# Second and fourth attention pair in buffers borrowed from the gelu products

## The chip, the cores and the metric

One Trainium2 chip (trn2), one of its cores. The metric is the device time of one execution in microseconds (us), median of the runs; every run quoted was of the fast state or, being on one core, judged against the fastest of its kernel. A ratio is the mean time of one kernel's fast runs over the mean of the other's fast runs of the same rounds, so it is not quite the ratio of the medians quoted beside it. All profile figures are from one profiled execution of each kernel, whose span is some 2 us shorter than the run's time.

## The reference, cut to what matters

```python
# q, k, v: (8 batches, 8 heads, 576, 64) float32
scores = scale * np.matmul(q, k.transpose(0, 1, 3, 2))
thresh = np.max(scores, axis=-1, keepdims=True) - tau
scores = np.where(scores >= thresh, scores, -1e9)
attn   = softmax(scores)                       # exp, sum, divide
x      = (attn @ v), heads side by side        # (4608, 512)
h      = x @ w_in                              # w_in (512, 2048), float64 in memory
g      = h / (1 + np.exp(-1.702 * h))
out    = g @ w_out                             # w_out (2048, 512), float64 in memory
```

## The kernel before

Two heads make a pair, so there are 32 pairs; four pairs are one batch. The feed-forward part runs in nine blocks of 512 rows. The kernel is written as a list of tasks, each with an engine, an estimated cost, a rank, the tasks it comes after and the buffers it takes and gives back. A small simulation at build time starts, on each engine, the ready task of lowest rank whose buffers are free, and the instructions are issued in the order that results. On the chip each engine then keeps that order, so costs and buffer counts change nothing but order and space.

```python
limits = {"psA": 3, "psM": 2, "s_m": 7, "s_t": 2, "io": 3, "xT": 3, "mb": 1,
          "raw0": 1, "raw1": 1, "qkT0": 1, "qkT1": 1, "v_m": 2, "w64": 3, "cv": 2}
...
gT = [const.tile([P, BLK], FP32, name=f"gT{j}") for j in range(NFC)]   # 16 gelu products
kd = [const.tile([P, P], FP32, name=f"kd{i}") for i in range(2)]        # by n % 2
...
# 64 weight pieces, float64 to float32, rank 3.2 to 4.2
a = task("SP", 1.1, rank, load_w, i, take=("w64",), lag=3.5)
a = task("DVE", 0.6, rank, cv_open, i, after=[a], take=("cv",))
m = task("ACT", 0.42, rank, cv_mant, i, after=[a])
e = task("POOL", 0.82, rank, cv_exp, i, after=[a])
a = task("DVE", 0.42, rank, cv_sign, i, after=[e], give=("w64",))
ready_w.append(task("POOL", 0.75, rank, cv_end, i, after=[a, m], give=("cv",)))
...
# pair n, rank n (cut): transposes, scores in 4 tiles and a tail, row maxima,
# subtract (DVE), mask and exponential (ACT), sums and values (PE), place (DVE)
pq = task("DVE", 0.78, r, prep, n, 0, after=[lq], take=("qkT0",), give=("raw0",))
a  = task("PE", ..., scores, n, t, after=[pq, pk] + ..., take=("psA", "psA", "s_m"),
          give=("qkT0", "qkT1") if tail else ())
```

In the traces, `ps` are scores, `s_m` score tiles, `part` the row maxima of a tile, `mb` the spread maxima, `den` and `pv` sums and values, `hps` and `ops` the two feed-forward products. "DVE" is VectorE, "ACT" ScalarE, "POOL" GpSimd, "PE" TensorE.

Of the kernel before, what the change touches and what calls it, by code (L numbers as in the profile page):

```python
# [10 lines left out]
FP32 = mybir.dt.float32  # L11
# [3 lines left out]
ALU = mybir.AluOpType  # L15
# [3 lines left out]
P = 128  # L19
# [10 lines left out]
def kernel(  # L30
# [29 lines left out]
    nc = tc.nc  # L60
    B, H, S, D = q.shape
    d_model, d_ff = moe_w_in.shape
    NPAIR = H // 2
    NKT = 4
# [3 lines left out]
    QB = S // 32  # L68
    BLK = 512
    NBLK = B * S // BLK  # L70
    NDC = d_model // P
    NFC = d_ff // P
# [5 lines left out]
    const = ctx.enter_context(tc.tile_pool(name="const", bufs=1))  # L78
    work = ctx.enter_context(tc.tile_pool(name="work", bufs=2))
# [2 lines left out]

    w_in = const.tile([P, NDC, d_ff], FP32, name="w_in")
    w_out = const.tile([P, NFC, d_model], FP32, name="w_out")
    gT = [const.tile([P, BLK], FP32, name=f"gT{j}") for j in range(NFC)]
    kd = [const.tile([P, P], FP32, name=f"kd{i}") for i in range(2)]
    v_t = [const.tile([P, 2, D], FP32, name=f"v_t{i}") for i in range(2)]
    ones = const.tile([P, D], FP32, name="ones")
# [12 lines left out]
    tasks = []  # L101
    limits = {"psA": 3, "psM": 2, "s_m": 7, "s_t": 2, "io": 3, "xT": 3, "mb": 1,
              "raw0": 1, "raw1": 1, "qkT0": 1, "qkT1": 1, "v_m": 2, "w64": 3, "cv": 2}

    def task(engine, cost, rank, f, *a, after=(), take=(), give=(), lag=0.06):
        tasks.append((engine, cost, rank, f, a, [x for x in after if x is not None],
                      take, give, lag))
        return len(tasks) - 1
# [47 lines left out]
        assert started == len(tasks), (started, len(tasks))  # L156


    raws, vs = {}, {}

    def load_qk(n, which, queue):
        b, hp = divmod(n, NPAIR)
        name, src = (("q", q), ("k", k))[which]
        t = work.tile([P, QB, 32], FP32, name=f"{name}_raw", tag=f"{name}_raw", bufs=1)
        for h in range(2):
            for j in range(2):
                queue.dma_start(
                    out=t[ds(64 * h + 32 * j, 32), :, :],
                    in_=src[b, 2 * hp + h, :, ts(j, 32)].rearrange("(c p) d -> p c d", p=32),
                )  # L170
        raws[n, which] = t
# [18 lines left out]
    cv = {}  # L190
# [63 lines left out]
    mats, sT, stats, mbs, pss = {}, {}, {}, {}, {}  # L254

    def prep(n, which):

        dst = work.tile([P, S], FP32, name="qkT", tag=f"qkT{which}", bufs=1)
        nc.vector.transpose(out=dst, in_=raws.pop((n, which)).rearrange("p c d -> p (c d)"))  # L259
        mats[n, which] = dst  # L260

    def prep_kd(n):
# [29 lines left out]
    def keep(n, t, h):  # L292
        ps = pss[n, t][h]
        if t == NKT:
            st = work.tile([P, S], FP32, name="s_t", tag="s_t", bufs=2)
            o = st
        else:
            if h == 0:
                st = work.tile([P, 2, S], FP32, name="s_m", tag="s_m", bufs=7)
            else:  # L300
                st = sT[n, t]
            o = st[:, h, :]
        sT[n, t] = st
        nc.scalar.copy(out=halves(o), in_=ps[:, :, 0:SH])  # L304
# [43 lines left out]
        stats[n, ALU.max] = f  # L348

    def spread_max(n):  # L350
        mb = work.tile([P, 2, S], FP32, name="mb", tag="mb", bufs=1)
        nc.vector.transpose(  # L352
            out=mb.rearrange("p h s -> p (h s)"),
            in_=stats[n, ALU.max].unsqueeze(2).to_broadcast([P, 2 * QB, 32]),
        )
        mbs[n] = mb

    def sub(n, t):
        mb, s = mbs[n], sT[n, t]
# [173 lines left out]
    ready_w = []  # L533
    for i in range(len(pieces)):
        rank = NPAIR - 0.8 + i / len(pieces)
        if not wide:
            ready_w.append(task("SP", 0.6, rank, load_w, i, lag=2.5))
            continue
        a = task("SP", 1.1, rank, load_w, i, take=("w64",), lag=3.5)
        a = task("DVE", 0.6, rank, cv_open, i, after=[a], take=("cv",))  # L540
        m = task("ACT", 0.42, rank, cv_mant, i, after=[a])
        e = task("POOL", 0.82, rank, cv_exp, i, after=[a])
        a = task("DVE", 0.42, rank, cv_sign, i, after=[e], give=("w64",))
        ready_w.append(task("POOL", 0.75, rank, cv_end, i, after=[a, m], give=("cv",)))

    tau_done = task("DVE", 1.0, -2.0, tau_terms)

# [41 lines left out]
    for n in range(NP):  # L589
        gate = per_pair * (n - LEAD)  # L590
        after = ffn[gate : gate + 1] if gate >= 0 else []
        r = float(n)
        q0, q1 = (nc.sync, nc.scalar) if n == 0 else (nc.sync, nc.sync)
        lq = task("SP", 2.0, r - 2.0, load_qk, n, 0, q0, take=("raw0",), lag=2.0)
        lk = task("SP", 2.0 if n else 0.1, r - 2.0, load_qk, n, 1, q1, take=("raw1",), lag=2.0)
        lv = task("SP", 2.1, r - 1.2, load_v, n, take=("v_m",), lag=2.0)
        pq = task("DVE", 0.78, r, prep, n, 0, after=[lq], take=("qkT0",), give=("raw0",))
        pk = task("DVE", 0.78, r, prep, n, 1, after=[lk], take=("qkT1",), give=("raw1",))
        pd = task("ACT", 0.5, r, prep_kd, n, after=[pk])
        mx = []  # L600
        for t in range(NKT + 1):
            tail = t == NKT
            a = task(
                "PE", 1.1 if tail else 1.2, r, scores, n, t,
                after=[pq, pk] + ([pd] if tail else []) + after,
                take=("psA", "s_t") if tail else ("psA", "psA", "s_m"),
                give=("qkT0", "qkT1") if tail else (),
            )
            after = [a]
            c = [  # L610
                task("ACT", 0.64, r, keep, n, t, h, after=[a], give=("psA",))
                for h in range(1 if tail else 2)
            ]
            mx.append(task("DVE", 0.78 if tail else 1.37, r, in_groups, n, t, ALU.max, after=c))
        a = task("DVE", 0.75, r, over_tiles, n, ALU.max, after=mx)
        a = task("DVE", 0.75, r, over_groups, n, ALU.max, after=[a])
        a = task("DVE", 0.6, r, lower, n, after=[a, tau_done])
        m = task("DVE", 1.38, r, spread_max, n, after=[a], take=("mb",))
        ws, subs = [], [m]
        for t in range(NKT + 1):  # L620
            tail = t == NKT
            a = task(
                "DVE", 1.5 if tail else 1.37, r, sub, n, t, after=subs[-1:],
                give=("mb",) if tail else (),
            )
            subs.append(a)
            a = task("ACT", 0.7 if tail else 1.17, r, mask, n, t, after=[a])
            ws.append(task("ACT", 0.88 if tail else 1.36, r, exps, n, t, after=[a]))
        back = ("s_m",) * NKT + ("s_t",)
        every = range(NKT + 1)  # L630
        if n < NPAIR:

            pv = den = None
            for t in every:
                first = t == 0
                den = task(
                    "PE", 1.1, r, sums_by_pe, n, [t], True, after=[ws[t], den],
                    take=("psM", "psM") if first else (),
                )
                pv = task(  # L640
                    "PE", 1.1, r, values, n, [t], after=[ws[t], den, pv, lv],
                    take=("psA",) if first else (), give=(back[t],) if t < NKT else ("s_t", "v_m"),
                )
            a = task("DVE", 1.2, r, one_row, n, after=[den], give=("psM", "psM"))
        else:
            pv = task("PE", 5.0, r, values, n, every, after=ws + [lv], take=("psA",), give=("v_m",))
        if NPAIR <= n < BY_PE:
            a = task("PE", 5.2, r, sums_by_pe, n, every, False, after=ws + [pv], take=("psA",), give=back)
            a = task("DVE", 1.2, r, one_row, n, after=[a], give=("psA",))
        elif n >= BY_PE:  # L650
            su = [
                task("DVE", 0.78 if t == NKT else 1.37, r, in_groups, n, t, ALU.add, after=[ws[t]])
                for t in range(NKT + 1)
            ]
            a = task("DVE", 0.75, r, over_tiles, n, ALU.add, after=su + [pv], give=back)
            a = task("DVE", 0.75, r, over_groups, n, ALU.add, after=[a])
            a = task("DVE", 0.7, r, one_group, n, after=[a])
        a = task("DVE", 1.05, r, spread_sums, n, after=[a])
        b, hp = divmod(n, NPAIR)
        new = {(b * S + x) // BLK for x in cuts(b)[:-1]} if hp == 0 else set()  # L660
        if b:
            new -= {(b * S - 1) // BLK}
        placed[n] = task(
            "DVE", 0.9, r, place_x, n, after=[a, pv], take=("xT",) * len(new), give=("psA",)
        )
        while hp == NPAIR - 1 and (next_blk + 1) * BLK <= (b + 1) * S:
            feed_forward(next_blk)
            next_blk += 1
# [31 lines left out]
```

## Time and profile before

Median 1498.32 us of 3 runs (1497.54 to 1499.23); with a fourth it is 1498.03. Span of the profile 1495.0 us.

| stretch of the span before | what runs | fullest engine |
|---|---|---|
| 20 to 133 us | the first four pairs; weight pieces in the gaps | VectorE, 96.7 of 113 us |
| 133 to 264 us | rest of the weight pieces, first block, pairs 5 to 7 | none |
| 280 us to the end | blocks and attention interleaved | TensorE, 1211 of 1215 us |

### The profile page before, as it was taken

Reading aid. Unit: us, or ns where it says so; the run is one execution under the profiler, and the core shown is the slowest. Engines: PE = TensorE matmul, PEld = TensorE weight load, DVE = VectorE, ACT = ScalarE, POOL = GpSimd, SP = SyncE. Lnnn points to the kernel's source line nnn. Section 1 sums busy time; section 2 is a strip of 40 time slices with the busy share of each in tenths; the row PEclk is TensorE's granted clock in tenths of the full one; section 3 lists DMA queues with packets and bytes.
Section 4 is the critical chain, followed back from the end, with each engine's and each line's share of the span. In section 5 each row is a group of like instructions: output and inputs, shape, how many; then the busy total and the mean of one; then the engine's idle time right before and its main releaser. Section 6 shows DMA issues by size and latency. Waiting matters only on the chain.

```text
span 1495.0 us, 14337 instructions
## 1 busy us (share of the span) xinstructions
PE 1423.8 (95%) x5056; PEld 662.6 (44%) x5056; DVE 973.9 (65%) x1678; ACT 653.8 (44%) x917; POOL 124.5 (8%) x204
## 2 busy tenths in 40 slices
PE   5758897999999999999999999999999999999998
PEld 3424343444444444444444444444444444444443
DVE  6788786458888888888876787678767850110100
ACT  4655544445554555555544454445445530110100
POOL 1335666000000000000000000000000000000000
PEclk8888998999999999999999999999999999999999
DMA  6446666111112111111111111111110000000000
GB/s 121 110 115 178 184 200 185 39 31 28 28 31 47 39 24 24 38 38 24 24 38 32 31 25 31 38 32 24 31 31 22 1 7 14 7 7 14 7 7 21
DMA packets 214295, 72.22 MB, mean 48 GB/s; under 512 B 193232, under 2 KB 201424, under 8 KB 214224
## 3 DMA queue, kind: packets, MB, share of 16 engines
q1 hardware_dynamic: 211856, 71.02, 19.6%
q8 instruction: 40, 0.66, 0.2%
q10 hardware_dynamic: 2368, 0.30, 0.2%
q14 instruction: 31, 0.25, 0.1%
HBM read 61.84 MB, written 9.44 MB: 48 GB/s over the span
## 4 chain that ended last, share of the span: by engine, by line
PE 85%; DVE 6%; POOL 2%; ACT 2%; DMA 2%; issue 2%; SPq 1%; POOLq 0%; DVEq 0%; ACTq 0%
PE ops L486 33%; PE hps L467 30%; PE pv L388 10%; PE ps L285 9%; PE ps L276 2%; PE den L388 1%; POOL ex L232 1%; DMA w64s<-in_moe_w_out_dram 1%; DVE ex L241 1%; ACT s_m L374 1%; ACT s_m L370 1%; POOL ex L235 1%; DMA w64s<-in_moe_w_in_dram 1%; DVE part L318 1%; DVE qkT L259 1%
## 5 line engine op out<-in xcount | busy, mean ns | idle before, releaser
L486 PE MATMUL ops<-w_out,gT 128*128 128x512 f32 x1152 | 516.7, 600 | 10.8 <-POOL w_out L249 9.9
L467 PE MATMUL hps<-xT,w_in 128*128 128x512 f32 x1152 | 514.5, 598 | 4.0 <-DVE gT L478 2.5
L318 DVE TRANSPOSE_TENSOR_REDUCE part<-s_m 128x36 f32<-128x1152 f32 x224 | 304.1, 1367 | 152.7 <-ACT s_m L304 144.2
L486 PEld LDWEIGHTS ops<-w_out,gT 128*128 128x128 f32 x1152 | 213.9, 190 | 278.4 <-issue 260.2
L467 PEld LDWEIGHTS hps<-xT,w_in 128*128 128x128 f32 x1152 | 213.5, 190 | 269.8 <-issue 244.3
L304 ACT COPY s_m<-ps 128x576 f32<-128x576 f32 x256 | 152.4, 639 | 253.1 <-PE ps L285 252.7
L478 DVE SCALAR_TENSOR_TENSOR gT<-th,hps 128x512 f32<-128x512 f32 x144 | 97.2, 675 | 207.4 <-ACT th L475 207.1
L285 PE MATMUL ps<-qkT 64*128 64x288 f32 x1024 | 174.6, 456 | 28.7 <-DVE qkT L259 24.9
L361 DVE TENSOR_TENSOR s_m<-s_m,mb 128x1152 f32<-128x1152 f32 x128 | 171.4, 1365 | 0.5
L374 ACT ACTIVATE s_m<-s_m,shift,scl 128x1152 f32<-128x1152 f32 x128 | 168.9, 1340 | 0.6
L370 ACT ACTIVATE s_m<-s_m 128x1152 f32<-128x1152 f32 x128 | 145.2, 1156 | 45.3 <-DVE s_m L361 44.8
L475 ACT ACTIVATE th<-hps 128x512 f32<-128x512 f32 x144 | 85.3, 592 | 172.1 <-PE hps L467 171.7
L285 PEld LDWEIGHTS ps<-qkT 64*128 64x128 f32 x1024 | 98.7, 200 | 134.6 <-issue 52.9
L388 PE MATMUL pv<-s_m,v_m 128*64 128x288 f32 x1024 | 136.9, 417 | 0.4 <-ACT s_m L304 0.4
L493 ACT ACTIVATE osb<-ops 128x512 f32<-128x512 f32 x36 | 21.4, 595 | 218.8 <-PE ops L486 218.8
L388 PEld LDWEIGHTS pv<-s_m,v_m 128*64 128x64 f32 x1024 | 72.2, 140 | 68.1 <-issue 10.5
L388 PE MATMUL den<-s_m,ones 128*64 128x288 f32 x256 | 37.2, 430 | 23.5 <-ACT s_m L374 21.7
L226 ACT ACTIVATE mant<-frac 128x256 f32<-128x256 uint32 x64 | 26.0, 416 | 53.7 <-DVE frac L213 53.6
L364 DVE TENSOR_TENSOR s_t<-s_t,mb 64x576 f32<-64x576 f32 x64 | 49.2, 768 | 0.4
L241 DVE SCALAR_TENSOR_TENSOR ex<-w,ex 128x256 uint32<-128x256 uint32 x64 | 31.8, 498 | 21.5 <-POOL ex L235 21.3
L232 POOL TENSOR_SCALAR ex<-ex 128x256 uint32<-128x256 uint32 x64 | 39.5, 617 | 70.0 <-DVE ex L217 68.0
L352 DVE STREAM_TRANSPOSE mb<-thr 128x1152 f32<-128x1152 f32 x32 | 44.0, 1373 | 0.9
(47 smaller groups left out, 641.0 us busy)
## 6 DMA issues: line engine op xcount, KB each, us to landing
q_raw<-in_q_dram SPq DMA_DIRECT2D x128, 72.0 KB, 2.5
out_dram<-osb SPq DMA_DIRECT2D x36, 256.0 KB, 2.0
k_raw<-in_k_dram SPq DMA_DIRECT2D x124, 72.0 KB, 2.6
v_m<-in_v_dram SPq DMA_DIRECT2D x64, 128.0 KB, 2.5
w<-in_moe_w_in_dram SPq DMA_DIRECT2D x32, 256.0 KB, 3.3
w<-in_moe_w_out_dram SPq DMA_DIRECT2D x32, 256.0 KB, 3.5
w64s<-in_moe_w_in_dram SPq DMA_DIRECT2D x32, 255.6 KB, 3.6
w64s<-in_moe_w_out_dram SPq DMA_DIRECT2D x32, 255.6 KB, 3.8
```

Source lines behind the costliest of these rows:

```text
L232: nc.gpsimd.tensor_scalar(out=ex, in0=ex, scalar1=1150.0, scalar2=896.0, op0=ALU.min, op1=ALU.max)
L285: nc.tensor.matmul(ps[h][:, c, 0:SH], lhsT=kT[ts(h, D), ts(t, P)], rhs=qT[ts(h, D), ts(c, SH)], start=True, stop=True,)
L304: nc.scalar.copy(out=halves(o), in_=ps[:, :, 0:SH])
L318: nc.vector.tensor_reduce(out=o, in_=i, axis=AXL.X, op=op, apply_transpose=True)
L361: nc.vector.tensor_tensor(out=s, in0=s, in1=mb, op=ALU.subtract)
L370: nc.scalar.activation(out=s, in_=s, func=AF.Prelu, alpha=STEEP)
L374: nc.scalar.activation(out=s, in_=s, func=AF.Exp, scale=scl, bias=shift)
L388: nc.tensor.matmul(o[c][ts(h, D), 0:SH], lhsT=lhsT, rhs=rhs, start=(t == 0), stop=(t == NKT),)
L467: nc.tensor.matmul(hidden[j], lhsT=w_in[:, c, ts(j, P)], rhs=xTs[blk][:, c, :], start=(c == 0), stop=(c == NDC - 1),)
L475: nc.scalar.activation(out=ths[j], in_=hidden[j], func=AF.Tanh, scale=GELU_SCALE / 2)
L478: nc.vector.scalar_tensor_tensor(out=gT[j], in0=ths.pop(j), scalar=1.0, in1=hidden.pop(j), op0=ALU.add, op1=ALU.mult)
L486: nc.tensor.matmul(acc[i], lhsT=gT[j][:, ts(i, P)], rhs=w_out[:, j, :], start=(j == 0), stop=(j == NFC - 1),)
```

## The change

The second and fourth pair (n = 1 and 3) get raw q and k, their transposes, four score tiles and the spread maxima in the space of the 16 gelu products, which are first written when the fourth pair is done. Four costs in the model of a weight piece are brought nearer to what the trace measures. Core of the diff, the rest cut:

```diff
-    gT = [const.tile([P, BLK], FP32, name=f"gT{j}") for j in range(NFC)]
+    gT_all = const.tile([P, NFC, BLK], FP32, name="gT")
+    gT = [gT_all[:, j, :] for j in range(NFC)]
...
+    for x in ("raw0", "raw1", "qkT0", "qkT1", "mb"):
+        limits[x + "_apart"] = 1
+    limits["s_m_apart"] = NKT
...
+    APART = (1, 3)
+    def home(n, tag, size, name, bufs, key=None):
+        if n in APART:
+            o = offset[key or tag]
+            return spare[:, o : o + size]
+        return work.tile([P, size], FP32, name=name, tag=tag, bufs=bufs)
+
+    def own(n, *pools):
+        return tuple(x + "_apart" for x in pools) if n in APART else pools
...
-        a = task("DVE", 0.6, rank, cv_open, ...)
+        a = task("DVE", 0.66, rank, cv_open, ...)
-        e = task("POOL", 0.82, rank, cv_exp, ...)
+        e = task("POOL", 1.0, rank, cv_exp, ...)
-        a = task("DVE", 0.42, rank, cv_sign, ...)
+        a = task("DVE", 0.5, rank, cv_sign, ...)
-        ready_w.append(task("POOL", 0.75, rank, cv_end, ...))
+        ready_w.append(task("POOL", 0.9, rank, cv_end, ...))
...
-                take=("psA", "s_t") if tail else ("psA", "psA", "s_m"),
-                give=("qkT0", "qkT1") if tail else (),
+                take=("psA", "s_t") if tail else ("psA", "psA") + own(n, "s_m"),
+                give=own(n, "qkT0", "qkT1") if tail else (),
```

More of the change, by code (lines that the diff above doesn't have):

```diff
@@ L156, in run_in_order @@
         assert started == len(tasks), (started, len(tasks))
+    APART = (1, 3)
+    spare = gT_all.rearrange("p j t -> p (j t)")
+    offset = {"raw0": 0, "raw1": S, "qkT0": 2 * S, "qkT1": 3 * S, "mb": 4 * S}
+    offset.update({f"s_m{t}": (6 + 2 * t) * S for t in range(NKT)})
+    def home(n, tag, size, name, bufs, key=None):
[5 more added lines that the diff above has]
+        return tuple(x + "_apart" for x in pools) if n in APART else pools
     raws, vs = {}, {}
@@ L163, in load_qk @@
         name, src = (("q", q), ("k", k))[which]
-        t = work.tile([P, QB, 32], FP32, name=f"{name}_raw", tag=f"{name}_raw", bufs=1)
+        t = home(n, f"raw{which}", S, f"{name}_raw", 1)
+        blocks = t.rearrange("p (c d) -> p c d", d=32)
         for h in range(2):
@@ L167, in load_qk @@
                 queue.dma_start(
-                    out=t[ds(64 * h + 32 * j, 32), :, :],
+                    out=blocks[ds(64 * h + 32 * j, 32), :, :],
                     in_=src[b, 2 * hp + h, :, ts(j, 32)].rearrange("(c p) d -> p c d", p=32),
@@ L256, in prep @@
     def prep(n, which):
-        dst = work.tile([P, S], FP32, name="qkT", tag=f"qkT{which}", bufs=1)
-        nc.vector.transpose(out=dst, in_=raws.pop((n, which)).rearrange("p c d -> p (c d)"))
+        dst = home(n, f"qkT{which}", S, "qkT", 1)
+        nc.vector.transpose(out=dst, in_=raws.pop((n, which)))
         mats[n, which] = dst
@@ L298, in keep @@
             if h == 0:
-                st = work.tile([P, 2, S], FP32, name="s_m", tag="s_m", bufs=7)
+                st = home(n, "s_m", 2 * S, "s_m", 7, f"s_m{t}")
+                st = st.rearrange("p (h s) -> p h s", h=2)
             else:
@@ L350, in spread_max @@
     def spread_max(n):
-        mb = work.tile([P, 2, S], FP32, name="mb", tag="mb", bufs=1)
+        mb = home(n, "mb", 2 * S, "mb", 1)
         nc.vector.transpose(
-            out=mb.rearrange("p h s -> p (h s)"),
-            in_=stats[n, ALU.max].unsqueeze(2).to_broadcast([P, 2 * QB, 32]),
+            out=mb, in_=stats[n, ALU.max].unsqueeze(2).to_broadcast([P, 2 * QB, 32])
         )
-        mbs[n] = mb
+        mbs[n] = mb.rearrange("p (h s) -> p h s", h=2)
     def sub(n, t):
@@ L539 @@
         a = task("SP", 1.1, rank, load_w, i, take=("w64",), lag=3.5)
-        a = task("DVE", 0.6, rank, cv_open, i, after=[a], take=("cv",))
+        a = task("DVE", 0.66, rank, cv_open, i, after=[a], take=("cv",))
         m = task("ACT", 0.42, rank, cv_mant, i, after=[a])
-        e = task("POOL", 0.82, rank, cv_exp, i, after=[a])
-        a = task("DVE", 0.42, rank, cv_sign, i, after=[e], give=("w64",))
-        ready_w.append(task("POOL", 0.75, rank, cv_end, i, after=[a, m], give=("cv",)))
+        e = task("POOL", 1.0, rank, cv_exp, i, after=[a])
+        a = task("DVE", 0.5, rank, cv_sign, i, after=[e], give=("w64",))
+        ready_w.append(task("POOL", 0.9, rank, cv_end, i, after=[a, m], give=("cv",)))
     tau_done = task("DVE", 1.0, -2.0, tau_terms)
@@ L593 @@
         q0, q1 = (nc.sync, nc.scalar) if n == 0 else (nc.sync, nc.sync)
-        lq = task("SP", 2.0, r - 2.0, load_qk, n, 0, q0, take=("raw0",), lag=2.0)
-        lk = task("SP", 2.0 if n else 0.1, r - 2.0, load_qk, n, 1, q1, take=("raw1",), lag=2.0)
+        lq = task("SP", 2.0, r - 2.0, load_qk, n, 0, q0, take=own(n, "raw0"), lag=2.0)
+        lk = task("SP", 2.0 if n else 0.1, r - 2.0, load_qk, n, 1, q1, take=own(n, "raw1"), lag=2.0)
         lv = task("SP", 2.1, r - 1.2, load_v, n, take=("v_m",), lag=2.0)
-        pq = task("DVE", 0.78, r, prep, n, 0, after=[lq], take=("qkT0",), give=("raw0",))
-        pk = task("DVE", 0.78, r, prep, n, 1, after=[lk], take=("qkT1",), give=("raw1",))
+        pq = task("DVE", 0.78, r, prep, n, 0, after=[lq], take=own(n, "qkT0"), give=own(n, "raw0"))
+        pk = task("DVE", 0.78, r, prep, n, 1, after=[lk], take=own(n, "qkT1"), give=own(n, "raw1"))
         pd = task("ACT", 0.5, r, prep_kd, n, after=[pk])
@@ L617 @@
         a = task("DVE", 0.6, r, lower, n, after=[a, tau_done])
-        m = task("DVE", 1.38, r, spread_max, n, after=[a], take=("mb",))
+        m = task("DVE", 1.38, r, spread_max, n, after=[a], take=own(n, "mb"))
         ws, subs = [], [m]
@@ L623 @@
                 "DVE", 1.5 if tail else 1.37, r, sub, n, t, after=subs[-1:],
-                give=("mb",) if tail else (),
+                give=own(n, "mb") if tail else (),
             )
@@ L628 @@
             ws.append(task("ACT", 0.88 if tail else 1.36, r, exps, n, t, after=[a]))
-        back = ("s_m",) * NKT + ("s_t",)
+        back = own(n, "s_m") * NKT + ("s_t",)
         every = range(NKT + 1)
```

## The prediction

> **What bounds the kernel now.** I read the page first, its busy shares and its 40 slices, then the busy time of each engine in four stretches that I cut by what the matrix engine was fed with, then the waits of each stretch.
>
> ```profile
> PE 1423.8 (95%) x5056; PEld 662.6 (44%) x5056; DVE 973.9 (65%) x1678; ACT 653.8 (44%) x917; POOL 124.5 (8%) x204
> ...
> PE   5758897999999999999999999999999999999998
> ...
> DVE  6788786458888888888876787678767850110100
> ...
> PEclk8888998999999999999999999999999999999999
> ```
>
> TensorE is the bound of the kernel, but not of its first seven slices (about 280 us). There VectorE carries the higher digits, and the clock row shows that TensorE was not always granted its full clock.
>
> ```profile
> core 0: us, PE busy (x) PEld busy (x) DVE busy (x) ACT busy (x) POOL busy (x), PEclk, DMA share, GB/s
> 0.00:20.00 20.00, 9.18 (x36) 5.48 (x36) 7.61 (x13) 7.23 (x12) 1.33 (x12) 1.00 0.84 163
> 20.00:133.00 113.00, 76.27 (x449) 41.64 (x451) 96.66 (x182) 69.53 (x98) 42.05 (x57) 0.82 0.45 115
> 133.00:264.00 131.00, 111.40 (x409) 50.79 (x405) 104.01 (x222) 61.85 (x108) 80.88 (x135) 0.95 0.65 190
> 264.00:280.00 16.00, 15.75 (x48) 7.04 (x49) 13.08 (x21) 10.94 (x15) 0.20 (x1) 0.89 0.16 35
> 280.00:1495.00 1215.00, 1211.16 (x4120) 557.69 (x4118) 752.51 (x1244) 504.27 (x685) 0.00 (x0) 1.00 0.12 25
> ```
>
> The cuts: at 133 us the fourth pair is placed and the first feed-forward block may start; at 264 us GpSimd ends the last of the 64 weight pieces; from 280 us on TensorE is busy for 1211 of 1215 us at full clock. So nothing after about 270 us can be shortened by a change that leaves TensorE's work alone, as this one does. All gain has to come from reaching that point earlier, or with more TensorE work already done. Up to 133 us VectorE is 96.7 of 113 us busy (86%), TensorE 76.3 and at 0.82 of its clock, ScalarE 69.5: VectorE is the one that nearly fills the stretch. From 133 to 264 us no engine is full.
>
> The waits of VectorE from 20 to 133 us, and of TensorE from 0 to 280 us:
>
> ```profile
> DVE ex L241 <- POOL ex L235: 5.8, 9, 1.0
> DVE part L318 <- ACT s_m L304: 5.1, 7, 1.3
> DVE part_t L318 <- ACT s_t L304: 2.0, 2, 1.8
> ```
>
> ```profile
> PE ps L285 <- DVE qkT L259: 24.9, 5, 9.4
> PE den L388 <- ACT s_m L374: 21.7, 7, 12.5
> PE ops L486 <- POOL w_out L249: 9.9, 4, 5.7
> ```
>
> The five waits for qkT are the seams between pairs: 9.4 us at the start, which no buffer can help, then 15.5 us over four seams. q and k have one raw and one transposed buffer each, so pair n+1 is transposed only after the last scores of pair n, and the seven score buffers hold up the fourth tile of the second pair until the first pair's values are multiplied. That is what the change goes at.
>
> **What the Trainium skill says.** "Perfetto Trace Analysis", section Optimization Strategy, says that the same gap repeating on the engine that should be saturated can mean that there is not enough SBUF for the next tile. The seams at 22, 54, 82 and 125 us agree, with the reservation that the engine near saturation here is VectorE, whose own gaps are smaller. "SBUF — State Buffer", section Who interferes with whom, says that a VectorE instruction with two SBUF inputs contends with a GpSimd instruction that reads SBUF, and that one waits for the whole of the other. The trace agrees: GpSimd's ex took 0.40 us at its shortest but 1.44 us at 112.4 and 117.1 us, beside 1.35 us subtractions with two SBUF inputs. "TensorE: Matmul & The Clock Gate", section What's actually happening, says that an idle TensorE is clocked down and that activity releases it; the 0.82 of the stretch with the seams against 1.00 after 280 us fits.
>
> **The change part by part.**
>
> *Own buffers for the second and fourth pair.* No instruction is added or removed; q and k, their transposes, the four score tiles and the row of maxima of pairs 1 and 3 lie in the space of the 16 gelu products. These are first written after the fourth pair is placed, so the new reuse costs no wait. The pools double for the first four pairs: score tiles 7 to 11, the others 1 to 2. The second pair's q and k can be loaded right behind the first pair's v, and transposed in VectorE's gaps at 12 to 15 us in place of 18.7 and 21.3 us; its scores then start near 18.5 in place of 22.2 us. The third pair's transposes no longer wait for the second pair's scores (47 and 53 us before).
>
> What this is worth is set by VectorE, not by TensorE's 15.5 us. In the stretch of 113 us VectorE does 96.7 us. Weight work in it is 8.6 + 7.2 + 8.5 = 24.3 us for about 19.5 pieces (1.25 us each, from its three rows); some 3 us belong to the fifth pair; the rest, 69 us, is what the first four pairs still need. Idle are 16.3 us. If the deeper pools leave 4 us of it, the fourth pair is placed at 20 + 69 + 24 + 4 = 117 us with as many pieces converted, 16 us earlier than before. But pieces have a lower rank than these pairs, and a denser queue leaves them fewer turns, with GpSimd blocked more often. With 14 pieces converted the pairs end at 20 + 69 + 17.5 + 4, about 111 us.
>
> *Weight costs in the model.* Only the order changes: the sign step is laid later behind GpSimd's exponent step (model 0.82 to 1.0 us; the trace has 0.617 + 0.440 on average for its two instructions), the end step 0.75 to 0.9 (0.875 measured). VectorE waits for GpSimd 5.8 us in the first stretch and 15.4 us in the second; a wait is some 0.7 us, and the sign step moves 0.18 us later, so I put about 5 us of 21 saved.
>
> *When the pieces end.* In the second stretch 45 pieces take 131 us, 2.91 us each, though GpSimd needs only 1.93 us for one: it is a chain of loads, VectorE, GpSimd, VectorE, GpSimd with two pieces in flight, which this change does not deepen. Better order may make it 2.75 us (an estimate: 5 us of 131 off, and a little for the POOL order). That gives: 19 pieces done at 117 us, 45 left: 117 + 45 x 2.91 = 248, or 241 at 2.75. 14 pieces done at 111 us, 50 left: 256, or 248. Against 264 us: 16, 23, 8 and 16 us earlier; the middle is about 15. I take the attention work done ahead by then as unchanged: VectorE has the same share for pairs 4 and up. So TensorE's saturated part starts about 15 us earlier, and 1498.3 - 15 = 1483.
>
> **The rivals.** (1) *The conversion is the bound and the pairs' gain is given back.* If the pairs crowd out the pieces and GpSimd is blocked more, 10 pieces may be done at 107 us: 107 + 54 x 2.91 = 264, no gain from the pieces; only attention pulled ahead counts. For it: GpSimd waited 68 us for VectorE's opening step in the first 340 us, TensorE waited for w_out four times, 5.7 us at the longest. Against it: the trace has TensorE idle or slow for other reasons too. Time then: 1492 to 1500. (2) *The order comes out luckily.* The rounds in which TensorE stood 12.5 us for the fourth pair's first exponential vanish, clock recovers, and both stretches shrink: 25 to 35 us, so 1464 to 1473. For it: full-clock TensorE work up to 264 us is only about 177 us (7.2 pairs of scores at 5.65, 6.2 pairs of values and sums at 10, 39 feed-forward steps at 1.91, durations of the later stretch), so 87 us are lost there. Against it: VectorE has only 8 + 16 + 27 us idle in that time, and its work stays. (3) *A queue stalls.* One queue issues all loads in a fixed order; a weight load that waits for its buffer (35.5 us of such waits for the sign step up to 140 us) holds up q and k behind it, and a matter of order could cost 5 to 15 us. It would show as new waits for raw loads; time 1500 to 1510.
>
> **Range and chances.** Centre 1483, from 15 us off. The gain is bounded by VectorE's idle time, about 43 us after 20 us, of which I expect a third; the rivals reach from a gain of 35 to a loss of 10. Range 1466 to 1499. Over 2% faster needs 30 us, thus nearly the whole of rival (2): 0.13. Slower than 2% would need 30 us lost in a stretch that becomes less constrained: 0.03. Within 2%: 0.84.
>
> **What would show it.** Right: after about 265 us all as before, TensorE full at clock 1.00; the wait of scores for qkT down from 24.9 to about 12 us; VectorE over 93% busy between 20 us and the placing of the fourth pair, which falls at 111 to 117 us; the last w_out piece at 241 to 256 us; the period of a piece between 2.7 and 2.95 us. Wrong: the fourth pair placed after 125 us, or the last piece at 264 us or later with the end moved all the same (then what counted was attention done ahead), or a gap in TensorE after 280 us, where gelu products would wait for readers of the borrowed space.

## The result, and the profile after

Median 1483.99 us of 4 runs (1483.07 to 1485.07) against 1498.03 us before (4 runs); ratio 0.9905, 95% interval 0.9888 to 0.9923. That is 14 us or 1% faster. The results are correct.

The page of the kernel after, slices of 37.1 us:

```profile
span 1482.9 us, 14338 instructions
...
PE   4979966999999999999999999999999999999998
...
DVE  6998878668887887778877787678767840110200
...
PEclk8999987999999999999999999999999999999999
```

VectorE is at 9 and 9 in slices 2 and 3 where it was at 7 and 8. TensorE is still not full before slice 8. So the seam at which the program becomes TensorE's did not move forward.

Two waits of TensorE, kernel after, from 0 to 300 us (columns: total, times, longest):

```profile
PE ops L507 <- POOL w_out L270: 17.5, 5, 5.6
PE den L409 <- ACT s_m L395: 16.6, 3, 8.8
PE ps L306 <- DVE qkT L280: 15.8, 2, 9.3
```

The wait of scores for transposes fell from five to two: the start (9.3 us) and one at 233 us between later pairs. No seam among the first four pairs is left. The wait for w_out rose from 9.9 to 17.5 us. How the second pair's scores start, in the order of time, kernel before and then after:

```profile
22.17 6.99 PE L285 MATMUL ps<-qkT 64*128 64x288 f32 x24 [3.54 <-DVE qkT L259]
```

```profile
17.53 1.24 PE L297 MATMUL ps<-qkT,kd 128*128 128x288 f32 x4
18.70 1.81 PE L306 MATMUL ps<-gT 64*128 64x288 f32 x10
```

They follow the first pair's tail at once, out of the borrowed space (the name gT).

VectorE's busy time in stretches cut at the fourth pair's placing and at the last weight piece, kernel after:

```profile
core 0: us, PE busy (x) PEld busy (x) DVE busy (x) ACT busy (x) POOL busy (x), PEclk, DMA share, GB/s
20.00:108.80 88.80, 65.50 (x438) 37.21 (x435) 83.26 (x154) 66.46 (x87) 19.14 (x30) 0.90 0.36 90
108.80:269.82 161.02, 131.37 (x521) 60.98 (x522) 130.37 (x274) 81.06 (x137) 101.46 (x162) 0.90 0.67 194
```

The fourth pair is placed at 108.8 us, 25 us earlier than the 133.7 us before, and VectorE is busy for 83.3 of 88.8 us (94%, was 86%). But only ten weight pieces got their sign step in that stretch, where 19 had it before 133 us. After it, up to the last piece, VectorE is busy for 130.4 of 161.0 us (81%).

Now both kernels cut at the end of the last weight piece, before and then after:

```profile
0.00:264.19 264.19, 196.85 (x890) 97.90 (x890) 208.46 (x415) 138.60 (x218) 124.45 (x204) 0.90 0.58 156
264.19:1495.00 1230.81, 1226.91 (x4166) 564.72 (x4166) 765.39 (x1264) 515.21 (x699) 0.01 (x1) 1.00 0.12 25
```

```profile
0.00:269.82 269.82, 207.28 (x1001) 104.70 (x1002) 222.47 (x440) 155.13 (x238) 121.93 (x204) 0.91 0.58 155
269.82:1483.00 1213.18, 1209.35 (x4056) 556.40 (x4055) 750.40 (x1239) 500.48 (x681) 0.00 (x0) 1.00 0.12 25
```

This is the account of the gain in the two profiled executions (1496.9 and 1484.7 us; the medians differ by 14.0). The last piece ends 5.6 us **later** (269.8 against 264.2). But TensorE has 1209.4 us of work left then and not 1226.9, 17.6 us less. 17.6 - 5.6 = 12.0 us, and the spans differ by 12.1. What is done ahead is one pair of values and sums and one pair of scores, counted by their instructions (a pair has 80 of values and sums, and 32 of scores without its tail). Values and sums, then scores, before:

```profile
0.00:264.19 264.19, 68.40 (x480) 0.90 0.58 156
...
0.00:264.19 264.19, 49.87 (x224) 0.90 0.58 156
```

and after:

```profile
0.00:269.82 269.82, 78.56 (x560) 0.91 0.58 155
...
0.00:269.82 269.82, 47.49 (x256) 0.91 0.58 155
```

After the last piece the values and sums left take 131.9 us in place of 142.0, and the scores 119.1 in place of 124.7. That is 10.1 + 5.6 of the 17.6 us; the rest is small differences in work of the same kind.

And VectorE was idle up to the last piece for 264.19 - 208.46 = 55.7 us before and 269.82 - 222.47 = 47.4 us after. The fall is in the stretch from 20 us to the placing of the fourth pair (16.3 to 5.5 us); after the placing the idle time rose, from 27.0 to 30.6 us.

### The profile page after: what moved, and what is told of

Read it like the earlier page. It is cut to its first block, busy times and chain, and to the rows that moved or that the text cites. A ratio compares the mean times of both kernels' runs of the same rounds, so it can differ in the third digit from the quotient of the medians.

```text
span 1482.9 us, 14338 instructions
## 1 busy us (share of the span) xinstructions
PE 1416.6 (96%) x5056; PEld 661.1 (45%) x5056; DVE 972.9 (66%) x1678; ACT 655.6 (44%) x917; POOL 121.9 (8%) x204
## 4 chain that ended last, share of the span: by engine, by line
PE 87%; DVE 7%; POOL 2%; DMA 2%; issue 1%; ACT 1%; SPq 0%; DVEq 0%; POOLq 0%; ACTq 0%
PE ops L507 34%; PE hps L488 32%; PE pv L409 10%; PE ps L306 9%; PE ps L297 2%; PE den L409 1%; POOL ex L253 1%; DVE s_m L382 1%; DVE part L340 1%; DMA w64s<-in_moe_w_in_dram 1%; DVE ex L262 1%; POOL ex L256 1%; DMA w64s<-in_moe_w_out_dram 1%; DVE gT L382 1%; DVE mb L374 0%
## 5 line engine op out<-in xcount | busy, mean ns | idle before, releaser
L507 PE MATMUL ops<-w_out,gT 128*128 128x512 f32 x1152 | 518.7, 601 | 17.5 <-POOL w_out L270 17.5
L340 DVE TRANSPOSE_TENSOR_REDUCE part<-s_m 128x36 f32<-128x1152 f32 x216 | 293.3, 1368 | 157.7 <-ACT s_m L326 148.1
L326 ACT COPY s_m<-ps 128x576 f32<-128x576 f32 x240 | 142.2, 640 | 259.3 <-PE ps L306 259.2
L306 PE MATMUL ps<-qkT 64*128 64x288 f32 x960 | 155.4, 438 | 21.3 <-DVE qkT L280 15.8
L382 DVE TENSOR_TENSOR s_m<-s_m,mb 128x1152 f32<-128x1152 f32 x120 | 160.8, 1369 | 0.6
L391 ACT ACTIVATE s_m<-s_m 128x1152 f32<-128x1152 f32 x120 | 135.9, 1154 | 55.0 <-DVE s_m L382 54.7
L395 ACT ACTIVATE s_m<-s_m,shift,scl 128x1152 f32<-128x1152 f32 x120 | 158.4, 1338 | 0.7
L306 PEld LDWEIGHTS ps<-qkT 64*128 64x128 f32 x960 | 86.9, 190 | 116.8 <-ACT s_m L326 44.5
L409 PE MATMUL pv<-s_m,v_m 128*64 128x288 f32 x960 | 129.1, 421 | 0.0
L409 PE MATMUL den<-s_m,ones 128*64 128x288 f32 x192 | 28.0, 436 | 17.3 <-ACT s_m L395 16.6
L340 DVE TRANSPOSE_TENSOR_REDUCE part_t<-s_t 128x18 f32<-128x576 f32 x56 | 42.0, 750 | 1.1 <-ACT s_t L395 0.7
L262 DVE SCALAR_TENSOR_TENSOR ex<-w,ex 128x256 uint32<-128x256 uint32 x64 | 30.1, 475 | 19.0 <-POOL ex L256 18.6
```

What stands on the lines that cost most here:

```text
L306: nc.tensor.matmul(ps[h][:, c, 0:SH], lhsT=kT[ts(h, D), ts(t, P)], rhs=qT[ts(h, D), ts(c, SH)], start=True, stop=True,)
L326: nc.scalar.copy(out=halves(o), in_=ps[:, :, 0:SH])
L340: nc.vector.tensor_reduce(out=o, in_=i, axis=AXL.X, op=op, apply_transpose=True)
L382: nc.vector.tensor_tensor(out=s, in0=s, in1=mb, op=ALU.subtract)
L391: nc.scalar.activation(out=s, in_=s, func=AF.Prelu, alpha=STEEP)
L395: nc.scalar.activation(out=s, in_=s, func=AF.Exp, scale=scl, bias=shift)
```

## The experiments

Two theories stood at first. **Theory 1**: the buffers let VectorE run the first pairs without gaps, and the gain is what attention gets ahead by the last piece. **Rival**: the truer costs order the conversion better. Later runs set the first theory, in the form "VectorE's time up to the last piece sets the end", against the prediction's assumption that the chain of a weight piece does; they support it only for the stretch up to the placing of the fourth pair (see "More and less work on VectorE"). The change itself was not run again beside them; the kernel before was in every round, with medians of 1497.4 to 1498.4 us, so medians of different rounds can be compared to about 1 us. Of each run I took the same cut as above; the table gives all of them, in us.

| kernel | median | fourth pair placed | last piece L | VectorE idle before L | VectorE busy before L plus TensorE busy after L | values and sums before L |
|---|---|---|---|---|---|---|
| before | 1498.0 | 133.7 | 264.2 | 55.7 | 1435.4 | 480 |
| after | 1484.0 | 108.8 | 269.8 | 47.4 | 1431.8 | 560 |
| buffers only | 1488.7 | 111.8 | 267.9 | 50.8 | 1432.2 | 530 |
| costs only | 1498.8 | 136.7 | 265.6 | 52.6 | 1439.5 | 480 |
| second only | 1492.1 | 119.9 | 271.4 | 51.4 | 1433.0 | 560 |
| fourth only | 1489.0 | 95.7; the third, last here, 108.3 | 273.0 | 52.3 | 1430.2 | 560 |
| scores apart | 1490.8 | 115.4 | 274.8 | 53.3 | 1431.9 | 560 |
| q, k apart | 1494.2 | 128.4 | 278.0 | 56.7 | 1431.7 | 560 |
| lead 8 | 1485.9 | 108.3 | 268.1 | 46.2 | 1432.7 | 560 |
| deep (three pieces in flight) | 1489.9 | 108.6 | 267.6 | 46.1 | 1436.5 | 530 |
| double max | 1518.5 | 129.0 | 303.5 | 54.4 | 1459.0 | 560 |
| no sign | 1466.8 | 110.2 | 237.8 | 43.7 | 1417.5 | 480 |
| early | 1485.8 | 132.4 | 251.2 | 47.2 | 1431.7 | 480 |
| costs up | 1493.2 | 108.3 | 275.6 | 53.7 | 1432.7 | 560 |

The two columns before the last add up, with some 4 us of TensorE's small gaps after L, to the profiled span. That is arithmetic and shows no cause; the runs that change one thing do that. Each row is one execution. Up to its last piece the kernel with lead 8 runs the same order as the kernel after, so its differences (1.8 us in L, 0.9 us in the sum) show how much two executions scatter.

One figure that is not in the table hardly changes. From the moment when all of the first four pairs are placed to L, the pieces that are left take 2.87 to 3.13 us each in every kernel but the one without the sign step (2.50): 2.90 before, 2.98 after, 3.00 with three pieces in flight, 3.01 with double maxima, 2.90 with early pieces. VectorE was idle for 17 to 23% of that stretch in all of them, so it was not full there.

### Buffers without the costs

```diff
-        a = task("DVE", 0.66, ...); e = task("POOL", 1.0, ...)   # sign 0.5, end 0.9
+        a = task("DVE", 0.6, ...);  e = task("POOL", 0.82, ...)  # sign 0.42, end 0.75
```

> Own buffers as in the change, the weight steps' costs in the model as before. Theory 1 (the buffers close VectorE's gaps before the fourth pair is placed; one more pair of attention is done by the last weight piece): 1483 to 1488 us, fourth pair placed at 108 to 114 us. Rival (the truer costs order the conversion better, and this is the gain): 1494 to 1499 us. Both halves matter: near 1490.

1488.68 us (1488.5 to 1490.61), ratio 0.9938 (0.9923 to 0.9952): two thirds of the gain, just outside what theory 1 gave and 1.3 us from the 1490 of "both halves matter". The fourth pair is placed at 111.8 us, as it said.

### Costs without the buffers

The kernel before with the four new costs only.

> Buffers as before, only the four costs changed. Theory 1: 1495 to 1500 us, with VectorE's waits for GpSimd's exponent step down from 21 us by some 5 us at most and the fourth pair placed at 130 us or later. Rival (costs): 1482 to 1489 us.

1498.76 us, ratio 1.0004 (0.9988 to 1.0021). Alone the costs do nothing. VectorE's waits for the exponent step did fall from 21.3 to 16.7 us, about the 5 us predicted, and no time came of it. The rival falls as the main cause. Within the new buffers the costs seem to be worth the rest, 0.9938 to 0.9905, though those two intervals just touch.

### One of the two pairs alone

```diff
-    APART = (1, 3)
+    APART = (1,)          # second only
+    APART = (3,)          # fourth only
```

> Only the second pair in the borrowed space; the fourth in the shared pools. Theory 1 with each pair closing its own seam: about half the gain, 1489 to 1493 us. If the second pair's buffers alone matter because they unlock the third pair too: 1484 to 1487 us. Rival (costs, which are new here): 1484 as the whole change.

1492.13 us (1490.01 to 1492.35), ratio 0.9954 (0.994 to 0.9969): about half the gain, as theory 1 said; placed at 119.9 us.

> Only the fourth pair in the borrowed space. Theory 1: the first seam and the wait of the second pair's fourth score tile stay, so 1489 to 1495 us, placed at 118 to 126 us. Rival (costs): 1484 as the whole change.

1489.01 us, ratio 0.9936 (0.9921 to 0.9951), but with a **wrong result** (relative error 0.12), and the fourth pair placed at 95.7 us, not at 118 to 126, ahead of the third (108.3 us). The instruction order shows why the result is wrong: with buffers of its own and nobody ahead of it in them, the fourth pair's scores overtake the second's last ones. Both write the same block-diagonal tail of k (`kd`, two copies, chosen by n % 2), and the fourth's copy (at 25.9 us) comes before the second's tail scores have read it (at 48.0 us). So its time stands for another order of work, and I take no share of the gain from it. In the whole change the second and fourth pair share one apart set, and that keeps them in order.

### Which of the buffers

```diff
+    MINE = ("s_m", "mb")                          # scores apart
+    MINE = ("raw0", "raw1", "qkT0", "qkT1")       # q, k apart
-        if n in APART:
+        if n in APART and tag in MINE:            # and the same in own()
```

> Of the second and fourth pair only the four score tiles and the row of maxima lie apart; q, k and their transposes stay in the shared single buffers. If the score tiles are what held the pairs: 1484 to 1487 us. If the seams come from the transposes' single buffer (as the prediction said first): the gain is mostly lost, 1492 us or more.

1490.78 us (1490.73 to 1495.34), ratio 0.9967 (0.9946 to 0.9987): between the two expectations.

> Only q, k and their transposes lie apart; scores and maxima in the shared pools of seven and one. If the single transposed buffer made the seams: 1484 to 1488 us. If the seven score tiles hold the second pair up anyway: 1494 us or more. Both needed: both kernels of this pair near 1492 us or more.

1494.22 us, ratio 0.9981 (0.9966 to 0.9996). Neither half alone is near 0.9905; which of the two gives more is not settled, the intervals overlap. The seams take both: with q and k apart the second pair's last tile still comes late, behind the seven score tiles (its tail scores ran at 43.8 us, in the change at 24.9), and with the score tiles apart the scores still wait for the one transposed buffer (3.5 us at 21.9 us and 4.1 us at 70.1 us).

### More attention allowed ahead

```diff
-    LEAD = 6
+    LEAD = 8
```

> The change, with attention allowed two pairs further ahead of the feed-forward steps. In the kernel after, the last piece ends 6 us later than before and the time is what TensorE has left by then, so if more attention is available for VectorE and TensorE during the conversion: 1474 to 1480 us, with 8 or more pairs' values done by the last piece. If VectorE's time is what sets both: within 3 us of 1484.

1485.93 us (1483.16 to 1489.31), ratio 0.9925 (0.9905 to 0.9946): not faster than the change. In the traces TensorE, VectorE, ScalarE and GpSimd keep the order of the kernel after up to 397 us, so nothing up to the last piece was changed by the edit. The gate on attention was not what limited it there.

### Three weight pieces in flight

```diff
-              ... "w64": 3, "cv": 2}
+              ... "w64": 3, "cv": 3}      # frac and ex in three buffers
-        mant = work.tile([P, WC], FP32, name="mant", tag="mant")
+        mant = cv[i][1].bitcast(FP32)      # in place, to make room
```

> The change, with three weight pieces in flight in place of two (the mantissas written in place to make room). If the piece's own chain sets the end of the conversion, as the prediction's 2.91 us a piece assumed: last piece at 240 to 255 us and 1470 to 1478 us. If VectorE's time is the limit: the last piece ends earlier but as much attention is left over, within 3 us of 1484.

1489.91 us, ratio 0.9949 (0.9934 to 0.9964): slower than the change, by neither theory's number. The last piece ends at 267.6 us, only 2.2 us earlier, hardly more than the scatter of 1.8 us seen with lead 8, and a piece after the placing took 3.00 us against 2.98. So two pieces in flight were not what holds a piece; the three load buffers were not deepened, and VectorE's waits for loads of w_in went from 5.0 to 9.3 us.

### More and less work on VectorE

```diff
+        for _ in range(2 if n < NPAIR else 1):                       # double max
             nc.vector.tensor_reduce(out=o, in_=i, axis=AXL.X, op=op, apply_transpose=True)
```

> The change, with the row maxima of the first four pairs taken twice (same result): 25 us more of VectorE in the head (4 pairs x (4 x 1.37 + 0.78)), none in the chain of a weight piece and none on TensorE. If VectorE's filling up to the last piece sets the end: 1500 to 1510 us. If the chain of a piece does (the prediction's assumption): under 1490 us, as the pieces' own steps are the same.

1518.47 us, ratio 1.0138 (1.0122 to 1.0153), results correct. 25 us of VectorE that touch neither a weight piece nor TensorE's work cost 34 us, and the time is 8 us above the range of the first theory. The cut at its last piece:

```profile
0.00:303.46 303.46, 225.65 (x1006) 109.83 (x1006) 249.05 (x468) 157.35 (x239) 124.08 (x204) 0.86 0.50 138
303.46:1600.00 1296.54, 1209.94 (x4050) 557.14 (x4050) 747.25 (x1231) 499.46 (x678) 0.01 (x1) 1.00 0.11 24
```

TensorE has as much left as in the kernel after (1209.9 against 1209.4), but the last piece is 33.6 us later: 26.6 us more of VectorE's busy time and 7.1 us more of its idle time. The 33.6 us have three parts. The fourth pair is placed 20.2 us later (129.0 against 108.8), with VectorE 95% busy from 20 us on. Only 6 pieces are done by then and not 10, and four pieces at 2.98 us are 11.9 us. The last 1.5 us are a slightly slower piece, 3.01 us. So the run supports VectorE's time as the bound **up to the placing**, where the work was added, and there pieces lose their turns to the pairs. What limits a piece **after** the placing it does not test: a fixed time per piece, as the prediction assumed, fits as well as VectorE's time. Nor does it exclude that the second maximum acts through each pair's own chain.

```diff
-        e = task("POOL", 1.0, rank, cv_exp, i, after=[a])
-        a = task("DVE", 0.5, rank, cv_sign, i, after=[e], give=("w64",))
-        ready_w.append(task("POOL", 0.9, rank, cv_end, i, after=[a, m], give=("cv",)))
+        e = task("POOL", 1.0, rank, cv_exp, i, after=[a], give=("w64",))   # no sign
+        ready_w.append(task("POOL", 0.9, rank, cv_end, i, after=[e, m], give=("cv",)))
```

> The change without VectorE's sign step of each weight piece (results are wrong on purpose: all weights positive). It takes 30 us from VectorE and two hops from each piece's chain. If VectorE's time sets the end: 1455 to 1465 us. If GpSimd and the loads hold the pieces anyway: 1474 us or more, last piece after 255 us.

1466.81 us, ratio 0.9794 (0.9777 to 0.981), wrong result. The last piece ends at 237.8 us, 32 us earlier, as far as the 30 us taken from VectorE; but TensorE then has 14 us more left, so 17 us come out, just short of the range. After the placing a piece took 2.50 us in place of 2.98, less by about one sign step (0.47 us). This run also frees the load buffers earlier and shortens a piece's chain, so by itself it does not tell VectorE's time from the chain.

### Weight pieces earlier

```diff
-        rank = NPAIR - 0.8 + i / len(pieces)
+        rank = NPAIR - 1.8 + i / len(pieces)
```

> The change with the weight pieces ranked one pair earlier (they take turns from the third pair on in place of the fourth). If the last piece is not the lever but VectorE's whole filling: last piece earlier by 5 us or more, more of TensorE's work left, and the time within 4 us of 1484. If the last piece is the lever: 1475 to 1479 us.

1485.82 us (1483.36 to 1487.49), ratio 0.9918 (0.9903 to 0.9934): the time of the change, by the other road. The cut at its last piece:

```profile
0.00:251.17 251.17, 187.95 (x884) 94.91 (x884) 204.00 (x411) 137.53 (x215) 124.31 (x204) 0.90 0.59 163
251.17:1600.00 1348.83, 1227.66 (x4174) 565.43 (x4172) 768.96 (x1268) 517.20 (x702) 0.00 (x1) 1.00 0.11 23
```

The last piece is 18.7 us earlier than in the kernel after, and TensorE has 18.3 us more left. VectorE's idle time is the same, 47.2 against 47.4 us. It is the clearest run: pieces done in the first stretch and attention were exchanged one for one, and the end of the pieces by itself is not a lever.

### Costs raised once more

```diff
-  0.66 / 1.0 / 0.5 / 0.9      +  0.75 / 1.2 / 0.6 / 1.05
```

> The change with the four weight costs in the model raised again by about as much (0.75, 1.2, 0.6, 1.05), now above what the trace measures. If truer costs are what gave 4.7 us between the buffers alone and the whole: 1486 to 1490 us. If the longer spacing of the chain is: 1480 to 1484 us. If any change of order moves the time by some us, it may land anywhere from 1480 to 1490.

1493.21 us, ratio 0.9969 (0.9954 to 0.9983): outside all the ranges. Too high is worse than too low. VectorE's waits up to the last piece, in the order old costs (the buffers-only kernel), the change, raised:

```profile
DVE ex L262 <- POOL ex L256: 27.5, 38, 1.6
...
DVE frac L234 <- DMA w64s<-in_moe_w_out_dram: 2.5, 3, 1.4
DVE frac L234 <- DMA w64s<-in_moe_w_in_dram: 2.1, 3, 1.1
```

```profile
DVE ex L262 <- POOL ex L256: 18.6, 30, 1.6
DVE frac L234 <- DMA w64s<-in_moe_w_out_dram: 5.9, 5, 2.2
DVE frac L234 <- DMA w64s<-in_moe_w_in_dram: 5.0, 5, 1.5
```

```profile
DVE ex L262 <- POOL ex L256: 13.1, 19, 1.6
DVE frac L234 <- DMA w64s<-in_moe_w_out_dram: 10.3, 8, 2.3
DVE frac L234 <- DMA w64s<-in_moe_w_in_dram: 8.0, 7, 2.0
```

A later sign step waits less for GpSimd and gives its load buffer back later, so the next piece's first step waits for its load: 27.5 + 4.6, 18.6 + 10.9, 13.1 + 18.3, in sum 32, 29.5 and 31 us. That trade is read from the waits, not tested by itself, and the sums explain only 2 to 3 of the 5 to 9 us; the rest is the order of other work and stays open.

No version tried was faster than the change with right results.

## Why the prediction was right, and where its road was wrong

The time (1483 said, 1484 measured) was right, and so was most of its first half; the second half named a road that the kernel did not take.

- *The bound and the seams*: right. After the last piece all is as before, and no gap for the borrowed space appears. The second pair's scores start at 18.7 us (18.5 said). The waits for transposes among the first four pairs are gone; the sum came down to 15.8 and not 12 us, because one new wait of 6.5 us stands at 233 us.
- *VectorE sets the first stretch*: right. It was to be over 93% busy (94%) and to leave 4 us idle (88.8 - 83.3 = 5.5).
- *Fourth pair placed at 111 to 117 us with 14 to 19 pieces*: **the count failed.** It was 108.8 us with 10 pieces, which is the "107 us with 10" of rival (1). The term mis-sized is the number of turns that a denser queue leaves to pieces of lower rank.
- *GpSimd blocked more often*: not seen. Up to the placing its first exponent step took 568 ns on average after and 706 before, over all pieces 591 and 617.
- *Costs of the model save 5 us*: of the waits yes, with the old buffers (21.3 to 16.7 us); of the time no (ratio 1.0004).
- *When the pieces end*: **this step failed, through the count and hardly through the pace.** It said a last piece at 241 to 256 us. Measured: 54 pieces from 108.8 to 269.8 us, 2.98 us each, just above its range of 2.7 to 2.95. Against its case of 14 pieces at 111 us and 2.91 us a piece, the end is 13.3 us later: 11.9 for four more pieces, 3.6 for the pace, less 2.2 for the earlier placing. Its reason for the pace, two pieces in flight, is not borne out (3.00 us with three). What does set the pace is open: VectorE was 81% busy in that stretch, the load buffers were not deepened, and the one run that changed the pace took a step from VectorE and from the piece's chain at once.
- *Attention done ahead taken as unchanged*: **failed with it.** It is where the gain is: one more pair of values and sums and one more pair of scores, 17.6 us of TensorE's work with the small rest, less the 5.6 us that the last piece is later. The prediction had named this among the signs against it ("then what counted was attention done ahead").
- That the two errors nearly cancel has a reason in part: pieces done early and attention done early were exchanged one for one. The run with early pieces took the prediction's road (last piece at 251 us, attention as before) and arrived at the same time. That the number came out within 1 us is luck in part. The prediction bounded the gain by VectorE's idle time and expected a third of 43 us; the idle time up to the last piece fell by 8.4 us, and 3.6 us came from the other column of the table, of which no run tells the cause.
- *Rival (1)*: its road came true (10 pieces at the placing, the last piece no earlier, only attention pulled ahead counts). Its time, 1492 to 1500 us, did not, because that attention was worth 17.6 us.
- *Rivals (2) and (3)*: did not occur. TensorE's longest wait for an exponential went from 12.5 to 8.8 us, but its waits for w_out grew.
- Three readings in the prediction are loose. Seven slices are 262 us and not 280. VectorE's 8 us idle before 20 us are 12.4 by its own line (20.00 - 7.61). And its lines fit the clock only in part: in the first 20 us the clock was 1.00 with TensorE busy for 9.2 us.

## What to carry to other kernels

Where a stretch feeds a saturated engine through another one that is nearly full, count the second one's idle time up to the hand-over and the first one's work left after it: a milestone that comes earlier is worth nothing if it was paid with work left over. Work added to an engine in one stretch tells of the limit in that stretch alone; here the pace of the pieces after it stayed at about 3 us. Space that is empty until a known point is good for doubling single buffers before that point, but both halves of a chain need it (here transposes and score tiles) to close a seam. A pool of one may be the only thing that keeps two users of some other buffer in order: doubling it for one of them alone gave wrong results here.

## What the Trainium skill lacked or had wrong

- "Perfetto Trace Analysis", section Optimization Strategy, says to find the gaps of the engine one optimizes and what blocks it. It lacks a way to weigh, where one stretch feeds the next, an earlier hand-over against work left after it. Here the last piece came 5.6 us later with 17.6 us less left, and the gaps of the bounding engine misled: TensorE's wait for w_out rose from 9.9 to 17.5 us while the time fell by 14 us, and VectorE's idle time up to the last piece fell from 55.7 to 47.4 us.
- "SBUF — State Buffer", section Who interferes with whom, was right on who waits (GpSimd's step 0.40 us at its shortest, 1.44 us beside subtractions with two SBUF inputs). It has no figure for a mixed stretch: on average 0.57 us after and 0.71 us before, up to the placing of the fourth pair, so a denser VectorE did not block GpSimd more here.
- No page that I read has what costs in a build-time order do to in-order queues: at too low, measured and too high costs VectorE waited 27.5, 18.6 and 13.1 us for GpSimd and 4.6, 10.9 and 18.3 us for loads, and the middle was fastest (1488.7, 1484.0, 1493.2 us).
- No page that I read warns that a buffer count can be what keeps order for a different buffer: the fourth pair alone in space of its own gave a relative error of 0.12.
